# Block means of batch 0's values: eight narrow copies become two wide ones, and tile 0's second copy changes engine

## Chip, cores, metric

One core of a Trainium2 chip. The metric is the device time of one execution in microseconds (us), lower is better; the kernel before takes 511.47 us, the median of three runs (511.29 to 512.98). A core has a matrix engine (TensorE, PE in the profile, with its weight loads as PEld), a vector engine (VectorE, DVE), a scalar engine (ScalarE, ACT), a general one (GpSimd, POOL) and a queue that here only issues transfers (SyncE, SP). Each runs its own instructions in order, and waits on semaphores that the others raise.

## The reference, cut down

Attention over a local window plus block summaries, then two feed-forward parts:

```python
k_sum = k.reshape(B, H, nb, block, D).max(axis=3)
v_sum = v.reshape(B, H, nb, block, D).mean(axis=3)      # block = 32, nb = 24
scores_l = where(|i - j| < 16, scale * q @ k^T, -1e9)
scores_s = scale * q @ k_sum^T + log(block)
a = softmax(concat([scores_l, scores_s]))
x = a @ concat([v, v_sum])                              # 2 batches, 768 rows, 8 heads x 64
x = sigmoid(xr @ w_r) * (relu(xk @ w_k) ** 2 @ w_v)     # xk, xr mix each row with the one before
u = x + (relu(x^T @ w_tok1) @ w_tok2)^T
out = u + relu(u @ w_ch1) @ w_ch2
```

## The kernel before

Attention works on 6 tiles of 128 rows in each of 2 batches. A tile's scores (`s_stage`, L309) go, for each half tile of 64 queries, against 96 window keys and the 24 block maxima. DVE adds the mask and takes the minimum (L327, into `pe`), ACT takes the exponential (L329). In batch 0 the division comes at the end (L377 to L386); in batch 1 DVE makes the reciprocals (L337, L338) and POOL scales `pe` by them (L340). TensorE transposes `pe` (L346, into bank `pt`), ACT or DVE copies it out as `PT` (L349, L351), and `v_stage` (L366) multiplies it with the values.

The values that `v_stage` reads are one 120-row operand for each half tile: 96 rows of v by DMA and, above or below them, the 24 block means. In batch 0 these operands lie in `ybuf`, slot 2t for tile t's first half (means in rows 0 to 23) and slot 2t + 1 for its second (rows 96 to 119). The means themselves are made once for a batch: DVE sums blocks (L253), TensorE transposes (L260), ACT scales into `vs` (L262). `copy_sums` (L278) then puts `vs` into each operand. In batch 0 ACT copies both of tile 0 (L283), and for each of tiles 1 to 5 POOL copies one (L287) and DVE the other (L285). In batch 1 it is a DMA (L281).

Beside attention runs the first feed-forward part, `main` (L523): `ko` matmuls (L477), ReLU on ACT (L489), square on DVE (L490), a split into a high part on ACT (L491, `kh`) and a low part on POOL (L492, `kl`), and `acc` matmuls (L477). All of these matmuls are three products of high and low parts. Each weight tile is prepared by ACT (L148), DVE (L152, L158), ACT again (L160, the high part) and POOL (L161, the low part); two buffers `wf` carry it, so the L152 of a weight waits for the L161 of the second-last one. `mixed` (L461) makes the inputs `xk` on POOL and DVE (L466, L467), with a high part on ACT (L468) and a low one on DVE (L469, `xl`).

The order on each engine is not the order of the code. `attention()` and `main()` are interleaved by a credit of costs, and a scheduler then orders every engine's instructions by priorities (`ahead(...)`) and its own estimate of when each is ready; a few matmuls and weight steps are tied to one another with `behind` and `after`. Score banks (`s`) and transpose banks (`pt`) are two each, bank `ko` is one. Eight short runs of idle matmuls (`spin`, L556) stand between the first score tiles.

Of the kernel before, what the change touches and what calls it, by code (L numbers as in the profile page):

```python
# [54 lines left out]
def fused_kernel(ctx, tc, q, k, v, vt, mu, w_k, w_v, w_r, w_t1, w_t2, w_c1, w_c2, out):  # L55
    nc = tc.nc
    B, NT = q.shape[:2]
    S, DM = v.shape[1] - WINDOW * 2, v.shape[2]
# [5 lines left out]
    NB = S // BLOCK  # L64
    KD = DM // 128
    PAD = 16
    NK = 96
    NC = NB + NK
# [21 lines left out]
    ybuf = ypool.tile([128, B * NT, DM], F32, name="ybuf")  # L90
# [4 lines left out]
    r1 = pool("r1", "right")  # L95
# [114 lines left out]
    state = {}  # L210
# [64 lines left out]
    def vw_sums(b, t):  # L275
        ahead(HV if b or t == 0 else 0)(copy_sums)(b, t)

    def copy_sums(b, t):  # L278
        for j, (w, srow) in enumerate(state[b]["vw"][t]):
            if b:  # L280
                nc.sync.dma_start(w[srow:srow + NB], state[b]["vs"])  # L281
            elif t == 0:
                nc.scalar.copy(w[srow:srow + NB], state[b]["vs"])  # L283
            elif j:
                nc.vector.tensor_copy(w[srow:srow + NB], state[b]["vs"])  # L285
            else:
                nc.gpsimd.tensor_copy(w[srow:srow + NB], state[b]["vs"])  # L287

    @ahead(HL)
    def q_load(b, t):  # L290
# [575 lines left out]
```

## Time and profile before

| what | value |
|---|---|
| median of 3 runs | 511.47 us |
| profiled execution, its time | 511.19 us |
| its span | 509.4 us |
| TensorE matmul busy | 492.6 us (97%) |
| DVE, ACT, POOL busy | 249.1, 206.4, 186.4 us |

The span is the stretch in which the program's instructions run; 1.8 us lie around it. Busy shares are means over stages: attention fills the first 170 us, and the second feed-forward part and its matmuls the rest. A wait counts only where TensorE stands idle for it.

### The profile page before, as it was taken

The page shows a single profiled execution, that of the slowest core. Times are in us where ns is not written, and L with a number is a line of the kernel's source. Part 1 is how long each engine was busy: PE and PEld are TensorE (multiplying, and loading weights), DVE is VectorE, ACT ScalarE, POOL GpSimd, SP SyncE. Part 2 cuts the span into 40 slices and gives each one's busy share as a digit, 9 for nine tenths or more (in the row PEclk, how much of TensorE's full clock was granted, in tenths as well). Part 3 has the DMA queues.
Part 4 walks back from the last instruction along what each step waited for, and adds up shares of the span by engine and source line. Part 5 has one row for each costly group of instructions (what it writes and reads, how often), then busy time and mean ns, then how long its engine had stood idle before and what let it go on. Part 6 is the DMA issues. An engine that isn't in the chain of part 4 may idle for free.

```text
span 509.4 us, 7950 instructions
## 1 busy us (share of the span) xinstructions
PE 492.6 (97%) x3064; PEld 399.6 (78%) x3064; DVE 249.1 (49%) x544; ACT 206.4 (41%) x477; POOL 186.4 (37%) x250
## 2 busy tenths in 40 slices
PE   7999897999999999999999999999999999999995
PEld 3578775788888888887888888888888888888884
DVE  3789999740515174798676576343141211311112
ACT  1689655962534444556455435343110201001000
POOL 5335567971534465697734333332100000000000
PEclk9999999999999999999999999999999999999999
DMA  8999942031000660001525650000020000200002
GB/s 254 307 295 338 333 128 71 9 100 40 21 0 14 237 248 0 1 0 42 164 85 209 235 176 1 0 1 1 0 84 0 1 0 1 82 1 0 0 1 82
DMA packets 24197, 45.40 MB, mean 89 GB/s; under 512 B 2112, under 2 KB 11328, under 8 KB 24160
## 3 DMA queue, kind: packets, MB, share of 16 engines
q1 hardware_dynamic: 24160, 44.90, 28.1%
q8 instruction: 24, 0.39, 0.3%
q14 instruction: 13, 0.11, 0.1%
HBM read 41.16 MB, written 3.15 MB: 87 GB/s over the span
## 4 chain that ended last, share of the span: by engine, by line
PE 79%; DVE 9%; POOL 4%; issue 3%; ACT 2%; DMA 2%; SPq 1%; DVEq 0%; POOLq 0%; ACTq 0%
PE o L791 19%; PE go L477 19%; PE ko L477 10%; PE acc L477 10%; PE ro L477 5%; PE ho L477 3%; PE h L477 3%; PE sp L309 3%; PE pv L366 2%; DVE xk L467 2%; PE pt L346 2%; DMA xT<-in_vt_dram 1%; PE spin L556 1%; DVE wf L152 1%; PE utr L745 1%
## 5 line engine op out<-in xcount | busy, mean ns | idle before, releaser
L477 PE MATMUL go<-u,w 128*128 128x512 f32 x432 | 106.7, 393 | 0.0
L161 POOL TENSOR_TENSOR w<-wf,w 128x512 fp32r<-128x512 f32 x50 | 68.7, 1379 | 85.5 <-ACT w L160 78.8
L477 PEld LDWEIGHTS go<-u,w 128*128 128x128 f32 x432 | 80.7, 188 | 17.5
L791 PE MATMUL o<-w,gh 128*128 128x512 f32 x288 | 89.0, 395 | 0.0
L706 DVE SCALAR_TENSOR_TENSOR gl<-go,gh 128x512 fp32r<-128x512 f32 x36 | 24.9, 691 | 121.1 <-ACT gh L705 120.9
L477 PE MATMUL ko<-xh,w 128*128 128x256 f32 x384 | 77.0, 289 | 0.7 <-ACT w L160 0.6
L705 ACT ACTIVATE gh<-go 128x512 fp32r<-128x512 f32 x36 | 21.5, 597 | 128.8 <-PE go L477 128.7
L477 PEld LDWEIGHTS ko<-xh,w 128*128 128x128 f32 x384 | 61.4, 188 | 4.5 <-issue 1.3
L791 PEld LDWEIGHTS o<-w,gh 128*128 128x128 f32 x288 | 54.0, 188 | 12.1
L477 PE MATMUL acc<-w,kh 128*128 128x512 f32 x192 | 60.7, 398 | 1.9 <-ACT kh L491 1.9
L477 PE MATMUL ko<-xl,w 128*128 128x256 f32 x192 | 54.6, 284 | 1.0 <-DVE xl L469 1.0
L791 PE MATMUL o<-w,gl 128*128 128x512 f32 x144 | 55.4, 394 | 0.0
L160 ACT CAST w<-wf 128x512 fp32r<-128x512 f32 x50 | 30.9, 619 | 47.3 <-DVE wf L158 47.1
L492 POOL TENSOR_TENSOR kl<-rl,kh 128x512 fp32r<-128x512 f32 x24 | 34.5, 1437 | 34.6 <-ACT kh L491 31.2
L466 POOL TENSOR_SCALAR tmp<-xT,oms 128x256 f32<-128x256 f32 x52 | 38.1, 742 | 23.1 <-DVE xk L467 15.0
L158 DVE SCALAR_TENSOR_TENSOR wf<-wst,wf 128x512 int32<-128x512 int32 x50 | 41.4, 834 | 8.4 <-ACT wst L148 6.9
L329 ACT ACTIVATE pe<-pe,mn 128x120 f32<-128x120 f32 x96 | 36.6, 383 | 18.5 <-DVE mn L327 18.2
L477 PEld LDWEIGHTS acc<-w,kh 128*128 128x128 f32 x192 | 34.6, 188 | 9.1 <-ACT kh L491 2.4
L490 DVE TENSOR_TENSOR rl<-rl 128x512 f32<-128x512 f32 x24 | 18.9, 785 | 46.7 <-ACT rl L489 46.3
L467 DVE SCALAR_TENSOR_TENSOR xk<-xT,mus,tmp 128x256 f32<-128x256 f32 x52 | 39.2, 784 | 4.2 <-POOL tmp L466 3.8
L477 PE MATMUL acc<-w,kl 128*128 128x512 f32 x96 | 37.1, 397 | 1.1 <-POOL kl L492 1.1
L477 PEld LDWEIGHTS ko<-xl,w 128*128 128x128 f32 x192 | 36.2, 189 | 2.1 <-DVE xl L469 1.3
(85 smaller groups left out, 695.2 us busy)
## 6 DMA issues: line engine op xcount, KB each, us to landing
wst<-in_moe_w_ch_dram SPq DMA_DIRECT2D x24, 512.0 KB, 4.6
wst<-in_moe_w_k_dram SPq DMA_DIRECT2D x8, 512.0 KB, 7.6
wst<-in_moe_w_v_dram SPq DMA_DIRECT2D x8, 512.0 KB, 10.3
kw<-in_k_dram SPq DMA_DIRECT2D x12, 320.0 KB, 8.8
wst<-in_moe_w_tok_dram SPq DMA_DIRECT2D x6, 512.0 KB, 4.5
out_dram<-o SPq DMA_DIRECT2D x12, 256.0 KB, 2.0
ybuf<-in_v_dram SPq DMA_DIRECT2D x12, 192.0 KB, 9.8
vw<-in_v_dram SPq DMA_DIRECT2D x12, 192.0 KB, 2.6
```

What stands on the lines that cost most here:

```text
L158: nc.vector.scalar_tensor_tensor(wi, top, 3, wi, ALU.logical_shift_left, ALU.bitwise_or)
L160: self.rounded.append(nc.scalar.copy(hi, wf))
L161: nc.gpsimd.tensor_tensor(lo, wf, hi.bitcast(F32), ALU.subtract)
L329: nc.scalar.activation(pe, pe, AF.Exp, bias=mn[:, p:p + 1], scale=-1.0, accum_out=den[:, p:p + 1])
L466: nc.gpsimd.tensor_scalar(tmp, xT[:, d, x0 - 1:x0 - 1 + MW], om[:, d:d + 1], 1.0, ALU.mult, ALU.mult)
L467: nc.vector.scalar_tensor_tensor(xk[:, d], xT[:, d, x0:x0 + MW], mu[:, d:d + 1], tmp, ALU.mult, ALU.add)
L477: nc.tensor.matmul(o, l, r, start=(first and i == 0), stop=(last and i == 3 * n - 1))
L490: nc.vector.tensor_tensor(rl, rl, rl, ALU.mult)
L492: nc.gpsimd.tensor_tensor(lo, rl, hi.bitcast(F32), ALU.subtract)
L705: nc.scalar.activation(hi, o, AF.Relu)
L706: nc.vector.scalar_tensor_tensor(lo, o, 0.0, hi.bitcast(F32), ALU.max, ALU.subtract)
L791: nc.tensor.matmul(acc[t], l, r, start=(f == 0 and i == 0), stop=(f == nf - 1 and i == 2))
```

## The change

For batch 0, tile 0's first copy stays on ACT and its second goes to DVE; tile 1 keeps one copy on POOL and one on DVE. The copies of tiles 2 to 5 become two instructions, issued where tile 2's were: POOL writes the first-half slots of all four tiles (24 rows, 4 x 512 elements, `vs` read four times over), DVE the second-half slots. Batch 1 keeps its DMAs.

```diff
     def copy_sums(b, t):
-        for j, (w, srow) in enumerate(state[b]["vw"][t]):
-            if b:
-                nc.sync.dma_start(w[srow:srow + NB], state[b]["vs"])
-            elif t == 0:
-                nc.scalar.copy(w[srow:srow + NB], state[b]["vs"])
-            elif j:
-                nc.vector.tensor_copy(w[srow:srow + NB], state[b]["vs"])
-            else:
-                nc.gpsimd.tensor_copy(w[srow:srow + NB], state[b]["vs"])
+        vs = state[b]["vs"]
+        if b:
+            for w, srow in state[b]["vw"][t]:
+                nc.sync.dma_start(w[srow:srow + NB], vs)
+        elif t < 2:
+            (w0, r0), (w1, r1) = state[b]["vw"][t]
+            (nc.gpsimd.tensor_copy if t else nc.scalar.copy)(w0[r0:r0 + NB], vs)
+            nc.vector.tensor_copy(w1[r1:r1 + NB], vs)
+        elif t == 2:
+            rest = ybuf[:, 2 * t:2 * NT].rearrange("p (t two) n -> p t two n", two=2)
+            wide = vs.unsqueeze(1).to_broadcast([NB, NT - t, DM])
+            nc.gpsimd.tensor_copy(rest[0:NB, :, 0], wide)
+            nc.vector.tensor_copy(rest[NK:NC, :, 1], wide)
```

Behind line 292 the changed kernel's line numbers are 4 higher, so its L331 is L327 of before, its L494 is L490. On every engine the scheduler's order is another one, in places from about 28 us of the trace of before up to the end of attention. Three places follow.

ACT, as batch 0's last two tiles end. Before, the first ReLU of `main` (L489) stands behind the last two copies of attention:

```order
L160 CAST w<-wf 128x512
L148 ACTIVATE wst<-wst 128x512
L349 COPY PT<-pt 120x512
L385 COPY xT<-pv 128x4x128
L160 CAST w<-wf 128x512
L148 ACTIVATE wst<-wst 128x512
L489 ACTIVATE rl<-ko 128x512
```

With the change it stands ahead of them:

```order
L160 CAST w<-wf 128x512
L148 ACTIVATE wst<-wst 128x512
L493 ACTIVATE rl<-ko 128x512
L353 COPY PT<-pt 120x512
L389 COPY xT<-pv 128x4x128
L160 CAST w<-wf 128x512
L148 ACTIVATE wst<-wst 128x512
L495 CAST kh<-rl 128x512
```

The ReLU and the high part `kh` behind it have moved ahead, and so has the square on DVE (L490).

DVE, where batch 1's attention starts: the block maxima (L231) and what stands between them and the first masked scores of batch 1 (L327), before:

```order
L231 TENSOR_REDUCE ks<-kw 128x4x4 x2
L469 TENSOR_TENSOR xl<-xk,xh 128x1024
L231 TENSOR_REDUCE ks<-kw 128x4x4
L152 TENSOR_SCALAR wf<-wst 128x512
L158 SCALAR_TENSOR_TENSOR wf<-wst,wf 128x512
L351 COPY PT<-pt 120x512
L490 TENSOR_TENSOR rl<-rl 128x512
L253 TENSOR_REDUCE vrs<-ybuf 128x48
L158 SCALAR_TENSOR_TENSOR wf<-wst,wf 128x512
L152 TENSOR_SCALAR wf<-wst 128x512
L158 SCALAR_TENSOR_TENSOR wf<-wst,wf 128x512
L386 TENSOR_TENSOR xT<-xT,rb 128x4x128
```

And with the change:

```order
L231 TENSOR_REDUCE ks<-kw 128x4x4 x2
L473 TENSOR_TENSOR xl<-xk,xh 128x1024
L494 TENSOR_TENSOR rl<-rl 128x512
L158 SCALAR_TENSOR_TENSOR wf<-wst,wf 128x512
L152 TENSOR_SCALAR wf<-wst 128x512
L253 TENSOR_REDUCE vrs<-ybuf 128x48
L355 COPY PT<-pt 120x512
L158 SCALAR_TENSOR_TENSOR wf<-wst,wf 128x512
L331 ISA pe,mn<-sp,mask_183 128x120
L331 ISA mn 128x1
```

The last block maximum has moved ahead of the long `xl`, and the masked scores (8 pairs of such rows) ahead of two L152, one L158 and the L386.

TensorE, behind the scores of batch 1's second tile, before:

```order
L309 MATMUL sp<-kw,qT 64x120 x6
L477 MATMUL acc<-w,kh 128x512 x4
L477 MATMUL ko<-xh,w 128x256
L477 MATMUL ko<-xl,w 128x256
L477 MATMUL acc<-w,kl 128x512 x2
L477 MATMUL acc<-w,kh 128x512 x2
L477 MATMUL acc<-w,kl 128x512
L477 MATMUL acc<-w,kh 128x512 x2
L477 MATMUL acc<-w,kl 128x512
L309 MATMUL sp<-kw,qT 64x120
L346 MATMUL pt<-ident,pe 120x128 x4
```

And with the change:

```order
L313 MATMUL sp<-kw,qT 64x120 x16
L350 MATMUL pt<-ident,pe 120x128 x4
L313 MATMUL sp<-kw,qT 64x120
L350 MATMUL pt<-ident,pe 120x128
L481 MATMUL ko<-xh,w 128x256
L481 MATMUL ko<-xl,w 128x256
L350 MATMUL pt<-ident,pe 120x128 x2
L313 MATMUL sp<-kw,qT 64x120 x15
```

The first transposes of batch 1 now stand right behind the scores; the `acc` matmuls that separated them come later, and behind the rows shown follow 7 `ko` matmuls, one transpose, one score matmul of the fourth tile, 4 `acc` matmuls and 11 more scores of that tile.

## Rows read from the trace of the kernel before

**Rows 1.** Busy time by stretches: stretch, length, busy us (instructions) of PE, PEld, DVE, ACT, POOL; granted clock.

```profile
20.00:40.00 20.00, 20.00 (x219) 13.59 (x217) 15.61 (x62) 17.92 (x61) 8.83 (x10) 1.00 1.08 301
100.00:200.00 100.00, 100.00 (x827) 85.90 (x821) 41.18 (x105) 47.25 (x113) 51.13 (x68) 1.00 0.25 84
```

**Rows 2.** Timeline, TensorE's waits from 50 us: start us, length us, engine, line, [idle <-releaser].

```profile
53.20 0.39 PE L477 MATMUL ko<-xl,w 128*128 128x256 f32 x1 [1.04 <-DVE xl L469]
61.76 1.12 PE L556 MATMUL spin<-ident 128*128 128x512 f32 x2 [0.41 <-ACT rl L489]
67.56 1.19 PE L477 MATMUL acc<-w,kh 128*128 128x512 f32 x4 [0.84 <-ACT kh L491]
81.45 0.39 PE L309 MATMUL sp<-kw,qT 64*64 64x120 f32 x2 [0.87 <-issue]
82.22 0.82 PE L309 MATMUL sp<-kw,qT 64*64 64x120 f32 x18 [0.38 <-DVE mn L327]
86.26 1.20 PE L477 MATMUL acc<-w,kh 128*128 128x512 f32 x4 [1.05 <-ACT kh L491]
88.08 0.38 PE L477 MATMUL ko<-xh,w 128*128 128x256 f32 x1 [0.62 <-ACT w L160]
95.27 1.00 PE L346 MATMUL pt<-ident,pe 128*120 128x128 f32 x3 [0.28 <-POOL pe L340]
```

**Rows 3.** Timeline around the copies, as in rows 2.

```profile
22.70 3.42 DVE L285 COPY ybuf<-vs 24x512 f32<-24x512 f32 x5 [0.89 <-ACT vs L262]
22.73 3.85 POOL L287 COPY ybuf<-vs 24x512 f32<-24x512 f32 x5 [2.04 <-ACT vs L262]
24.09 1.24 ACT L283 COPY ybuf<-vs 24x512 f32<-24x512 f32 x2
27.38 0.68 DVE L351 COPY PT<-pt 120x512 f32<-120x512 f32 x1
28.48 0.97 PE L366 MATMUL pv<-PT,ybuf 120*64 120x64 f32 x13
```

**Rows 4.** The copies by tile `vs`: shortest/median/longest ns of one.

```profile
L285 DVE COPY ybuf<-vs x5: 420/826/827, 22.7 to 25.3; 24x512 f32<-24x512 f32 x5
L287 POOL COPY ybuf<-vs x5: 797/797/852, 22.7 to 25.8; 24x512 f32<-24x512 f32 x5
```

**Rows 5.** Timeline, DVE and POOL where batch 1 starts.

```profile
70.64 3.88 POOL L237 TENSOR_SCALAR kw<-ks 128x96 f32<-128x96 f32 x12 [1.77 <-DVE ks L231]
...
76.24 1.48 DVE L152 TENSOR_SCALAR wf<-wst 128x512 int32<-128x512 int32 x1 [1.19 <-POOL w L161]
77.82 1.60 DVE L158 SCALAR_TENSOR_TENSOR wf<-wst,wf 128x512 int32<-128x512 int32 x1
79.34 0.67 DVE L386 TENSOR_TENSOR xT<-xT,rb 128x512 f32<-128x512 f32 x1
...
80.35 0.60 DVE L152 TENSOR_SCALAR wf<-wst 128x512 int32<-128x512 int32 x1
82.08 0.73 DVE L467 SCALAR_TENSOR_TENSOR xk<-xT,mus,tmp 128x256 f32<-128x256 f32 x1
```

**Rows 6.** The chain that ended last, piece by piece: start us, length us, what.

```profile
83.04 1.61 PE ko L477 x12
84.65 0.58 PE sp L309 x12
```

**Rows 7.** Groups in 80 to 91 us: count, busy us, mean ns of one.

```profile
L467 DVE SCALAR_TENSOR_TENSOR xk<-xT,mus,tmp 128x256 f32<-128x256 f32 x4 | 3.4, 845 | 0.0
L158 DVE SCALAR_TENSOR_TENSOR wf<-wst,wf 128x512 int32<-128x512 int32 x3 | 3.2, 1053 | 0.0
...
L161 POOL TENSOR_TENSOR w<-wf,w 128x512 fp32r<-128x512 f32 x3 | 4.1, 1368 | 0.0
L466 POOL TENSOR_SCALAR tmp<-xT,oms 128x256 f32<-128x256 f32 x4 | 3.1, 770 | 2.1 <-DVE xT L386 1.3 <-DVE xk L467 0.7
L340 POOL TENSOR_SCALAR pe<-pe,den 128x120 f32<-128x120 f32 x4 | 2.0, 523 | 0.5 <-DVE den L338 0.5
```

## Prediction

> **What bounds the kernel now.** I read the shares by stretches first, then TensorE's waits on the timeline, then the stretch of the copies. From 100 to 200 us TensorE is busy all the time [rows 1], and it has little idle time behind that: what moves attention by a microsecond moves the end only if TensorE's waits before 100 us grow or shrink. From 50 us on the eight largest are 1.04, 0.41, 0.84, 0.87, 0.38, 1.05, 0.62 and 0.28, 5.5 us together [rows 2]. Each ends on DVE, ACT or POOL, none on a transfer. Between 20 and 40 us, where the copies are, TensorE is busy for 20.00 of 20 us at the full clock, 1.00 of 2.4 GHz [rows 1]: what DVE, ACT or POOL save there has no wait to shorten. So the copies can hardly gain by themselves. They can lose by coming late, and they gave the scheduler a reason to order attention anew, which is the larger part of this change.
>
> **The copies.** ACT loses one copy, 1.24 for two, so 0.6 [rows 3]; TensorE waits for nothing there, so it brings nothing. DVE gets six copies' worth of data in place of five, in three instructions; POOL keeps five, in two. Before, ten copies ran in pairs: POOL's five took 3.85, or 0.77 each, DVE's five 3.42 [rows 3]. One DVE copy took 0.42 and the others 0.83, though they are alike [rows 4]: a DVE copy waits out a POOL copy. The 0.77 of a pair holds a POOL part and a DVE part; the latter is at most 0.42, which leaves POOL 0.35 or more, and at most its 0.80. I take 0.45 and 0.32, because DVE's 0.42 holds a start that lies beside POOL's end.
>
> Now DVE's two narrow copies end at about 22.70 + 0.42 + 0.77 = 23.9. POOL's wide one has stood ready by then since its narrow copy ended (22.73 + 0.85 = 23.6), and goes first: 4 x 0.45 = 1.8, to 25.7. DVE's wide one follows, 4 x 0.32 = 1.3, to 27.0, where the block of before ended at 26.1. Behind it on DVE stand four masked scores, a weight step and the copy of PT, which ended at 28.06 and is read by the `pv` at 28.48 [rows 3]: slack 0.42. 0.9 later less 0.42 is a wait of 0.45 on TensorE. Ends: none, if DVE's wide copy goes first (23.9 + 1.3 = 25.2) or beside POOL's; 1.9, if POOL's part is all of its 0.80 (3.2, so 28.4). I take 0.45, since the pairs of before could not come every 0.77 with a part of 0.80.
>
> The Trainium skill speaks against the wide copies: "SBUF — State Buffer", section "SBUF: two separate sides", has DVE in its two-port mode and POOL take one port pair as an exclusive lock for a whole instruction, so four times the length locks the other out for four times as long. The alternating 0.42 and 0.83 agree [rows 4]. By that rule the sum holds the 0.45, and without it (side by side) it would be 0.45 lower.
>
> **The order from 50 to 82 us.** The first ReLU on ACT, its square on DVE and `kh` stand earlier; this ends the waits of 0.41 and 0.84 [rows 2]. The last block maximum stands ahead of `xl`, and the masked scores of batch 1's first tile ahead of L152, L158, L386 and L152; the waits of 0.87 and 0.38 of the second tile's scores on those go too [rows 2]. Together 2.50. The wait of 1.04 for `xl` halves, as `xl` now stands ahead of four masked scores, but four transposes that ran beside this wait (about 0.5, by the 1.00 of three that waited, an upper end) come afterwards: nothing. New: `kl` on POOL queues behind the twelve sums of 3.88 [rows 5], which start earlier but as one block; an estimate of 0.6, between 0 and 1.2. Net 2.50 - 0.6 - 0.45 = 1.45 gained when TensorE ends the second tile's scores. That was at 85.23 [rows 6], of which 1.61 was `ko` work that now comes later, so it is now 83.6 - 1.45 = 82.2.
>
> **The order from 82 to 100 us.** Here attention is pulled ahead of `main`. The waits of before there, 1.05, 0.62 and 0.28, lose their cause: 1.95 gone [rows 2]. But between the second tile's scores and the first transposes of batch 1 stood 20 matmuls that covered the way over DVE, ACT and POOL; now nothing does. I walk that way with the mean lengths of this stretch [rows 7].
>
> DVE ended the first tile's masked scores at 82.1; the 4.35 of L152, L158, L386 and L152 that stood ahead and 1.19 of idle time go [rows 5], the 0.9 of the copies comes: 77.5. Then two L152 (0.60) and two L158 (1.05), 3.3, to 80.8 with the reciprocals (small, left out). POOL scales four `pe` at 0.52, to 82.9: the four transposes end 0.3 late. DVE goes on with L386 and eight masked scores, 0.67 and 1.5 (82.08 less the end of L386, 80.01, less the 0.60 between), to 83.0. POOL does two L466 at 0.77, to 84.4, then the next `pe`, to 84.9: the next transpose, due at about 83.2, waits 1.7, and the two behind it some 0.4. TensorE then has 15 scores and 7 `ko` matmuls, about 2.1 by the paces of rows 6, and stands before the fourth tile's score at about 88.2. That needs DVE's third tile: from 83.0, two L467 at 0.85 and a square (taken as an L386, 0.67), 85.4; L152 waits until POOL's L161 returns its buffer (86.0 + 1.37 = 87.4), and with 0.60, L158's 1.05 and four masked scores of 0.75 it is 89.8: a wait of 1.6. Four `acc` matmuls of 1.2 later [rows 2] the other eleven scores wait for 0.75 + 0.60 + 0.85 on DVE, 92.0, where TensorE stands at 91.0: 1.0. Sum 0.3 + 1.7 + 0.4 + 1.6 + 1.0 = 5.0, the upper end. The lower is 0: with short lengths throughout DVE and POOL can be ahead. I take two thirds, 3.3, because the mean of 1.05 for an L158 comes from one long one among three. Net loss here 3.3 - 1.95 = 1.35. Behind that, `ko` matmuls cover everything again, as they did from 100 us on.
>
> **Sum.** The profiled execution took 511.19, 0.3 below the median of 511.47. 511.19 - 1.45 + 1.35 = **511.1**: no change that a measurement of this kernel could tell, which takes over 0.3% (1.5 us, so under 509.9 or over 513.0). With all ends low: 511.19 - 2.50 - 1.95 = 506.7; with all high (1.9, 1.2, 5.0): 511.19 - 2.50 - 1.95 + 8.1 = 514.8.
>
> **Rivals.** *Faster:* the early order pays and DVE keeps ahead, with new waits from 82 us on of 1.5 in place of 3.3: 509.3. For it: eight waits are known to go, while the new ones are worked out. Against: DVE is in the path of each new one. Chance 0.30.
>
> *Slower:* DVE's fixed order in 82 to 92 us. An L152 or L158 that meets POOL takes 1.48 or 1.60 against 0.60 [rows 5], and TensorE's third and fourth score tiles stand behind two of each. With two more long ones than I count, 2 x 0.95 on the upper end of 5.0, the sum is 511.1 + 1.7 + 1.9 = 514.7; it decides as soon as the new waits pass 5.2 (513.0). For it: nothing stands between to cover. Against: before, TensorE lost only 1.95 there beside the same instructions. Chance 0.22.
>
> *Long POOL copy:* POOL holds the port for 4 x 0.80 and the `pv` waits 1.9, not 0.45: 512.6. Against it: pairs every 0.77. Chance 0.08, still no change. The Trainium skill would give it: "GPSIMD Engine Reference", section "Elementwise — side-by-side cycle accounting", has 512 one-input elements at 769 ns, an estimate of 3.1 for the wide copy; rows 3 speak against it.
>
> **How the numbers follow.** Forecast 0.40 and the long copy 0.08 make no change 0.48; faster 0.30, slower 0.22. The range goes from 508.5, between the faster rival and the low end, to 513.6, between the threshold and the slower rival; about 0.1 is left out on each side.
>
> **What would show it.** Right: DVE's wide copy starts when POOL's ends and the block ends near 27.0; a wait of some 0.4 at the second `pv`; no wait at `spin` or the first `acc`; masked scores of batch 1's first tile done near 77.5; waits of transposes on L340 and of scores on L327 between 82 and 92; TensorE full behind 100. Wrong: new waits before 82 us, waits on a transfer of q or v for batch 1, or TensorE idle again behind 100 us.

## The result, and the profile after

The changed kernel takes 517.55 us (median of 5 runs, 515.16 to 520.07), the kernel before in the same session 511.47: a ratio of 1.0113 [1.0091, 1.0135]. It is slower by 1.1%, and above the range of 508.5 to 513.6. The profiled execution took 518.69, with a span of 516.9 us against 509.4. Executions of one kernel differ in their granted clock as well, and a trace is one of them: of eighteen of the kernel before, timed beside e5 to e7, the six with a mean clock of 0.998 took 510.9 to 511.6 us and the eight with 0.992 took 513.0 to 513.6.

The page of the changed kernel, first the span, then busy time of TensorE, then the granted clock in 40 slices of 12.9 us:

```profile
span 516.9 us, 7960 instructions
...
PE 497.5 (96%) x3064; PEld 404.3 (78%) x3064; DVE 248.3 (48%) x542; ACT 205.7 (40%) x476; POOL 185.0 (36%) x247
...
PEclk9999998799999999999999999999999999999999
```

TensorE ran the same 3064 matmuls. It was busy for 497.5 us, 4.9 more than before, and idle for 19.4, 2.6 more: together the 7.5 of the span. More busy time for the same work is new, and the row of the clock shows where: two slices of lower clock, from 77.5 to 103.4 us. The shares by stretches, TensorE alone (columns: stretch, its length, busy time and matmuls, granted clock, DMA share, GB/s):

```profile
70.50:73.80 3.30, 0.04 (x1) 1.00 0.01 2
73.80:75.20 1.40, 1.40 (x33) 1.00 0.00 0
75.20:82.00 6.80, 6.00 (x16) 0.50 0.00 0
82.00:93.00 11.00, 8.72 (x128) 1.00 0.41 115
93.00:95.70 2.70, 1.52 (x6) 1.00 0.00 0
95.70:102.50 6.80, 6.80 (x40) 0.50 0.00 0
```

Before, all of this was at 1.00. Now TensorE stands still from 70.5 to 73.8, and 1.4 us after it has started again it has 0.50, 1.2 GHz, for 6.8 us; then it has two waits between 91 and 95.7, and again 0.50 for 6.8 us. In the two stretches it was busy for 6.00 + 6.80 = 12.8 us, work of 6.4 at full clock: 6.4 us lost. With 2.6 of additional idle time that is 9.0, of which 1.5 came back elsewhere in TensorE's 497 us; that part was not traced.

TensorE's waits (who waits, for whom, us in total, times, longest):

```profile
PE sp L313 <- POOL kw L237: 4.4, 2, 3.3
PE sp L313 <- DVE mn L331: 3.0, 2, 1.8
PE acc L481 <- POOL kl L496: 1.9, 2, 1.1
...
PE pv L370 <- DVE PT L355: 0.6, 1, 0.6
PE ko L481 <- DVE xl L473: 0.5, 1, 0.5
...
PE sp L313 <- PE pt L350: 0.5, 1, 0.5
```

Of the eight waits of [rows 2] the one on `xl` is halved, and the other seven are gone. One of 3.3 us is new and far larger than any of them: batch 1's first scores wait for a sum of `kw` on POOL. (`ks` are the block maxima, the reference's `k_sum`; an instruction at L237 writes them beside the window keys in `kw`, twice for each tile, and the text calls these twelve instructions of a batch its sums. The other wait on `kw`, of 1.2, is batch 0's; `mn` are the minima that DVE writes as it masks the scores.) The timeline around it, POOL, then DVE, then TensorE (start, us, engine, line, operation, and in brackets the idle time before it and who ended it):

```profile
71.04 5.81 POOL L237 TENSOR_SCALAR kw<-ks 128x96 f32<-128x96 f32 x12
...
70.86 1.21 DVE L473 TENSOR_TENSOR xl<-xk,xh 128x1024 fp32r<-128x1024 f32 x1
72.00 0.68 DVE L494 TENSOR_TENSOR rl<-rl 128x512 f32<-128x512 f32 x1
72.60 0.68 DVE L158 SCALAR_TENSOR_TENSOR wf<-wst,wf 128x512 int32<-128x512 int32 x1
73.20 0.42 DVE L152 TENSOR_SCALAR wf<-wst 128x512 int32<-128x512 int32 x1
73.54 1.74 DVE L253 TENSOR_REDUCE vrs<-ybuf 128x48 f32<-128x1536 f32 x1
...
73.80 1.28 PE L313 MATMUL sp<-kw,qT 64*64 64x120 f32 x32 [3.26 <-POOL kw L237]
...
78.15 1.22 PE L481 MATMUL acc<-w,kl 128*128 128x512 f32 x2 [0.80 <-POOL kl L496]
```

And all sums of that line (duration in ns: least, median, longest):

```profile
L237 POOL TENSOR_SCALAR kw<-ks x24: 265/276/2710, 12.2 to 76.6; 128x96 f32<-128x96 f32 x24
```

23 of the 24 sums take about 0.27 us. The first of batch 1 takes 2.71: from 71.04 to 73.75, as long as DVE runs `xl`, the square `rl`, L158 and L152 without a pause; it ends when DVE has come to a reduction. Before, `xl` ran ahead of the last block maximum, and the twelve sums took 3.88 [rows 5], not 5.81, the longest of all sums 0.762.

Last the copies, DVE, POOL and the `pv` behind them, in the same columns:

```profile
24.49 2.91 DVE L291 COPY ybuf<-vs 24x2048 f32<-24x2048 f32 x1
...
24.23 2.08 POOL L290 COPY ybuf<-vs 24x2048 f32<-24x2048 f32 x1
...
29.39 0.97 PE L370 MATMUL pv<-PT,ybuf 120*64 120x64 f32 x13 [0.58 <-DVE PT L355]
```

POOL's wide copy goes first and ends at 26.31, DVE's ends 1.09 later: one after the other, as forecast, 2.08 and 1.09 where the forecast has 1.8 and 1.3, with a wait of 0.58 against the 0.45 forecast.

### The profile page after: what moved, and what is told of

Same layout as the page of the kernel before. It is cut to its first block, busy times and chain, and to the rows that moved or that the text cites. A ratio compares the mean times of both kernels' runs of the same rounds, so it can differ in the third digit from the quotient of the medians.

```text
span 516.9 us, 7960 instructions
## 1 busy us (share of the span) xinstructions
PE 497.5 (96%) x3064; PEld 404.3 (78%) x3064; DVE 248.3 (48%) x542; ACT 205.7 (40%) x476; POOL 185.0 (36%) x247
## 4 chain that ended last, share of the span: by engine, by line
PE 79%; DVE 11%; POOL 2%; DMA 2%; ACT 2%; issue 2%; SPq 1%; DVEq 0%; ACTq 0%
PE o L795 19%; PE go L481 19%; PE acc L481 12%; PE ko L481 11%; PE ro L481 4%; PE ho L481 3%; PE h L481 3%; PE pv L370 2%; DVE xk L471 2%; DMA xT<-in_vt_dram 2%; PE sp L313 2%; DVE pe L331 1%; PE pt L350 1%; DVE wf L152 1%; POOL kw L237 1%
## 5 line engine op out<-in xcount | busy, mean ns | idle before, releaser
L161 POOL TENSOR_TENSOR w<-wf,w 128x512 fp32r<-128x512 f32 x50 | 67.3, 1351 | 82.1 <-ACT w L160 79.5
L481 PE MATMUL acc<-w,kh 128*128 128x512 f32 x192 | 62.6, 415 | 0.0
L494 DVE TENSOR_TENSOR rl<-rl 128x512 f32<-128x512 f32 x24 | 19.6, 815 | 61.0 <-ACT rl L493 61.0
L158 DVE SCALAR_TENSOR_TENSOR wf<-wst,wf 128x512 int32<-128x512 int32 x50 | 40.7, 820 | 4.0 <-ACT wst L148 2.4
L481 PEld LDWEIGHTS acc<-w,kh 128*128 128x128 f32 x192 | 36.0, 196 | 7.8 <-issue 0.2
L481 PE MATMUL acc<-w,kl 128*128 128x512 f32 x96 | 38.5, 422 | 1.9 <-POOL kl L496 1.9
L471 DVE SCALAR_TENSOR_TENSOR xk<-xT,mus,tmp 128x256 f32<-128x256 f32 x52 | 35.6, 714 | 3.5 <-POOL tmp L470 3.2
```

The lines of the kernel that those rows point to most:

```text
L158: nc.vector.scalar_tensor_tensor(wi, top, 3, wi, ALU.logical_shift_left, ALU.bitwise_or)
L161: nc.gpsimd.tensor_tensor(lo, wf, hi.bitcast(F32), ALU.subtract)
L471: nc.vector.scalar_tensor_tensor(xk[:, d], xT[:, d, x0:x0 + MW], mu[:, d:d + 1], tmp, ALU.mult, ALU.add)
L481: nc.tensor.matmul(o, l, r, start=(first and i == 0), stop=(last and i == 3 * n - 1))
L494: nc.vector.tensor_tensor(rl, rl, rl, ALU.mult)
```

## The experiments

The theory after the result, **O**: not the copies but the new order costs the time. It puts four DVE instructions beside the first sum of `kw`, which holds the sum up; TensorE waits, and then loses its clock. Rivals: **W**, the wide copies cost it; **I**, the idle time alone counts and the clock falls for another reason; **V**, DVE's work sets this stretch whichever way TensorE waits. Each kernel was timed in 5 rounds beside the kernel before (511.4 to 512.9 us in these sessions). All of them:

| run | edit | us | ratio to before | mean clock |
|---|---|---|---|---|
| changed kernel | | 517.55 | 1.0113 [1.0091, 1.0135] | 0.985 |
| e1 | before, tile 0's second copy on DVE | 517.51 | 1.0095 [1.0071, 1.0118] | 0.984 |
| e2 | changed, wide copies cut up | 517.63 | 1.0102 [1.0084, 1.0120] | 0.981 |
| e3 | changed, last maximum behind `xl` | 521.32 | 1.0173 [1.0152, 1.0193] | 0.990 |
| e4 | changed, matmuls in the gap | 514.66 | 1.0045 [1.0029, 1.0062] | 0.993 |
| e5 | changed, two sums on ACT | 513.86 | 1.0034 [1.0015, 1.0054] | 0.987 |
| e6 | changed, tile 0 on ACT | 517.49 | 1.0099 [1.0074, 1.0124] | 0.985 |
| e7 | e6 and e5 together | 515.20 | 1.0059 [1.0036, 1.0082] | 0.990 |
| e8 | before, two tiles wide | 511.74 | 0.9997 [0.9984, 1.0010] | 0.996 |
| e9 | changed, twelve sums on ACT | 511.68 | 0.9988 [0.9974, 1.0001] | 0.991 |
| e10 | e5, later sums behind `kl` | 516.80 | 1.0089 [1.0070, 1.0108] | 0.990 |
| e11 | e9, two matmuls added | 511.37 | 0.9985 [0.9972, 0.9997] | 0.994 |
| e12 | e9, four matmuls added | 516.53 | 1.0094 [1.0076, 1.0111] | 0.998 |

**e1, e2 and e8: the order or the wide copies.** e1 takes the kernel before and moves one copy, from ACT to DVE:

```diff
-            elif t == 0:
+            elif t == 0 and j == 0:
                 nc.scalar.copy(w[srow:srow + NB], state[b]["vs"])
```

> The kernel before with one edit: tile 0's second block-mean copy on VectorE instead of ScalarE; the other ten copies stay narrow and where they were. Its instructions stand on every engine in the order of the changed kernel, but for the copies. Theory O (the loss is the new order: the first kw sum of batch 1 now runs beside two-input VectorE instructions and takes 2.7 us, TensorE waits 3.3 us at its scores and its granted clock then falls to 0.50): 515.5 to 518.5, a wait of 2.5 to 3.5 us at sp near 73 us, clock 0.50 for some 5 us after it. Theory W (the wide copies cost it, by holding SBUF or by delaying pv): 511 to 512, no such wait.

e2 takes the changed kernel and cuts its wide copies up:

```diff
-            nc.gpsimd.tensor_copy(rest[0:NB, :, 0], wide)
-            nc.vector.tensor_copy(rest[NK:NC, :, 1], wide)
+            for u in range(t, NT):
+                (w0, r0), (w1, r1) = state[b]["vw"][u]
+                nc.gpsimd.tensor_copy(w0[r0:r0 + NB], vs)
+                nc.vector.tensor_copy(w1[r1:r1 + NB], vs)
```

> The changed kernel with its two wide copies cut into four narrow ones each, at the same place and on the same engines; TensorE's and SyncE's orders are those of the changed kernel. Theory O: 515.5 to 518.5, as the changed kernel, with the same two stretches at clock 0.50; the wait at the second pv falls from 0.58 to under 0.5. Theory W: 511 to 512.5.

e8 is the kernel before, but for tiles 4 and 5, whose four narrow copies become two wide ones. The part of its kernel that makes them (cut: above it, tiles 0 to 3 are copied as before):

```python
        if t == 4:
            T = 4
            rest = ybuf[:, 2 * T:2 * NT].rearrange("p (t two) n -> p t two n", two=2)
            wide = vs.unsqueeze(1).to_broadcast([NB, NT - T, DM])
            nc.gpsimd.tensor_copy(rest[0:NB, :, 0], wide)
            nc.vector.tensor_copy(rest[NK:NC, :, 1], wide)
```

> The kernel before, with the copies of the last two tiles (not four) made by one wide instruction each on GpSimd and VectorE, issued with tile 4's; tiles 0 to 3 as before, so tile 0's two stay on ScalarE. TensorE's, ScalarE's and SyncE's orders are those of the kernel before. Theory O: as the kernel before, ratio 0.997 to 1.003, clock 1.00 from 60 to 120 us. Theory W (wide copies cost by themselves): 2 to 4 us slower, half of the change's loss for half of its wide tiles.

e1 has no wide copy and loses all the same; its trace has the sum of 2.71 and the wait again. In e2 they are there too, the sum with 2.71. e8 has wide copies, and no loss. The first two fences are the timelines of e1 and of e2, the third the shares of e8 by stretches, TensorE alone:

```profile
74.83 1.28 PE L309 MATMUL sp<-kw,qT 64*64 64x120 f32 x32 [3.26 <-POOL kw L237]
```

```profile
74.55 2.10 PE L313 MATMUL sp<-kw,qT 64*64 64x120 f32 x32 [3.27 <-POOL kw L237]
```

```profile
60.00:110.00 50.00, 45.33 (x440) 1.00 0.30 84
```

W has fallen: two wide tiles cost nothing that can be measured, and the changed kernel with its four is not slower than e1 and e2 without, as the intervals show. The wait of 0.58 behind the copies is gone in e2, as expected, and in e1; but both traces are at 0.50 from about 18 to 22 us, and TensorE comes to that place more than 1 us later, so this does not price the wide copies. e2's narrow copies end at 27.66, no earlier than the wide ones (27.40). The smallest part of the change is enough for the loss: one copy of tile 0 on another engine, from which the scheduler derives another order for the rest of attention. It is not the only part that is enough: in e6, below, the wide copies alone give a third order and a loss of the same size.

**e5 and e9: free the sums.** e5 takes the first two sums of batch 1 from POOL to ACT, and the order stays but for two places behind 90 us:

```diff
+            if b and t == 0:
+                nc.scalar.copy(st["kw"][t][:, :, o:o + NB], st["ks"])
+            else:
                 nc.gpsimd.tensor_scalar(st["kw"][t][:, :, o:o + NB], st["ks"], 1.0, 1.0, ALU.mult, ALU.mult)
```

> The changed kernel with batch 1's first two kw sums on ScalarE instead of GpSimd (which the two-input VectorE instructions beside them hold up); TensorE's, VectorE's and SyncE's orders stay but for two places after 90 us. Theory O: the first kw sum takes 0.3 to 0.5 us instead of 2.7, the wait at batch 1's first scores falls from 3.3 to 0.8 to 1.6 us, the granted clock stays 1.00 from 75 to 82 us: 2 us of waiting and some 3 us of half clock come back, 511.5 to 514. Rival V (VectorE's back-to-back work sets the time of this stretch, whichever way TensorE waits): the wait moves behind the scores (kl, mn), 515 to 517. Theory W (the wide copies): 517 to 518.

513.86, 3.7 less than the changed kernel: the total is inside O's range. But the clock is not as expected. e5's timeline, ACT, POOL, TensorE, and below it its sums on POOL:

```profile
71.09 0.45 ACT L238 COPY kw<-ks 128x96 f32<-128x96 f32 x2 [0.84 <-DVE ks L231]
...
71.22 4.76 POOL L240 TENSOR_SCALAR kw<-ks 128x96 f32<-128x96 f32 x10 [0.22 <-DVE ks L231]
75.95 1.78 POOL L499 TENSOR_TENSOR kl<-rl,kh 128x512 fp32r<-128x512 f32 x1
...
71.41 1.21 PE L316 MATMUL sp<-kw,qT 64*64 64x120 f32 x32 [0.76 <-ACT kw L238]
73.49 1.20 PE L484 MATMUL acc<-w,kh 128*128 128x512 f32 x4 [0.87 <-ACT kh L498]
...
77.78 1.22 PE L484 MATMUL acc<-w,kl 128*128 128x512 f32 x2 [2.85 <-POOL kl L499]
```

```profile
L240 POOL TENSOR_SCALAR kw<-ks x22: 268/272/2637, 11.5 to 75.7; 128x96 f32<-128x96 f32 x22
```

The scores wait 0.76, not 3.26. The hold-up has moved with the queue: the first sum that is left on POOL now takes 2.64, and `kl`, behind ten sums, is late by 2.85; the clock goes to 0.50 there (76 to 83 us). So e9 moves the other ten as well (the condition becomes `if b:`):

> The kernel of e5 with batch 1's other ten kw sums on ScalarE as well, so that none is left on GpSimd ahead of kl; the orders of TensorE and VectorE are those of e5. In e5 TensorE waited 2.85 us for that kl, which ten held-up sums (4.8 us) stood ahead of. Theory O: the sums take about 0.25 us each on ScalarE, kh comes 1 to 1.5 us later, kl 1 to 2 us earlier; the waits between 71 and 78 us fall from 4.5 to about 3.5 us in sum, none over 2.5, and the clock may stay 1.00: 510.5 to 513.5. Rival V (VectorE sets this stretch): 513.5 to 515, as e5.

511.68, a ratio of 0.9988 where the changed kernel has 1.0113: taking twelve small sums out of DVE's way gives back the whole loss. V has fallen. On ACT the twelve take 0.267 each; e9's timeline, ACT, POOL, TensorE:

```profile
70.28 2.17 ACT L238 COPY kw<-ks 128x96 f32<-128x96 f32 x12 [0.85 <-DVE ks L231]
...
73.05 1.30 POOL L499 TENSOR_TENSOR kl<-rl,kh 128x512 fp32r<-128x512 f32 x1 [2.85 <-ACT kh L498]
...
70.60 1.21 PE L316 MATMUL sp<-kw,qT 64*64 64x120 f32 x32 [0.76 <-ACT kw L238]
73.02 1.21 PE L484 MATMUL acc<-w,kh 128*128 128x512 f32 x4 [1.21 <-ACT kh L498]
```

With TensorE's and DVE's orders almost those of the changed kernel, its two later waits on `mn`, 1.79 and 1.18, are gone too: they came of the sums on POOL as well, by the late start or by POOL's longer queue, which no run tells apart. Not all of the clock is back: e9's trace keeps one stretch of 6.8 us at 0.50 (shown with e11), where the changed kernel has two; TensorE is idle for 14.1 us in it, in the kernel before for 16.8.

**e4: the clock by itself.** The sums stay held up; six matmuls of 256 columns fill the gap:

```diff
             nc.tensor.transpose(vp[:NB, p], st["vr"][:, p], ident)
+            if b and p == 1:
+                for _ in range(6):
+                    nc.tensor.matmul(vp[:, 2:4], ident, ident.unsqueeze(1).to_broadcast([128, 2, 128]), start=True, stop=True)
```

> The changed kernel with six additional matmuls of 256 columns on TensorE right ahead of batch 1's first scores (into a part of the bank that is overwritten later), some 2.6 us at full clock; the kw sums, xl and the copies are unchanged up to there, behind it the order differs. Theory O with the clock as its larger part: the first kw sum still takes about 2.7 us and the scores start no earlier, but TensorE is idle under 1.2 us there and its granted clock stays 1.00 from 75 to 82 us; 512.5 to 516. Rival I: the clock is 0.50 there all the same, 516 to 519. Theory W: 517 to 519.

514.66, 2.9 less than the changed kernel, with additional work on TensorE. Its shares by stretches, TensorE alone:

```profile
70.00:74.00 4.00, 3.33 (x30) 1.00 0.00 0
74.00:76.00 2.00, 1.25 (x13) 1.00 0.00 0
76.00:82.00 6.00, 5.02 (x49) 1.00 0.00 0
82.00:90.00 8.00, 4.67 (x27) 0.70 0.07 16
```

Its sums, and its wait at batch 1's first scores:

```profile
L237 POOL TENSOR_SCALAR kw<-ks x24: 268/272/2712, 11.8 to 75.4; 128x96 f32<-128x96 f32 x24
...
72.65 0.88 PE L316 MATMUL sp<-kw,qT 64*64 64x120 f32 x18 [0.67 <-POOL kw L237]
```

The first sum still takes as long, but TensorE waits 0.67, and from 76 to 82 us the clock is 1.00 where the changed kernel has 0.50. I has fallen for this stretch: with work in the place of the wait the clock stays. The other executions agree: the mean clock of e4's six is 0.990 to 0.995, of the changed kernel's five 0.982 to 0.989. Behind 82 us the order differs, a wait of 3.33 for a ReLU on ACT comes (82 to 90 us: busy 4.67 of 8), and with it a lower clock.

**e3: another order of the two.** The last block maximum goes behind `xl` instead of ahead of it (cut: `xls` collects the `xl` subtractions):

```diff
-        nc.vector.tensor_reduce(st["ks"][:, :, n * t:n * t + n], keys, AX.X, ALU.max)
+        m = nc.vector.tensor_reduce(st["ks"][:, :, n * t:n * t + n], keys, AX.X, ALU.max)
+        if b and t == NT - 1:
+            behind(m, xls[1:2])
```

> The changed kernel with VectorE's last key maximum of batch 1 put behind the 1.2 us xl subtraction instead of ahead of it, so that the kw sums start after xl; the copies are unchanged. Theory O: the first kw sum under 1.6 us, the wait at batch 1's first scores under 1.5 us, the granted clock 1.00 from 75 to 82 us; 511.5 to 515 (the later wait, on the maxima mn, may stay). Rival I (the idle time alone counts, the clock falls for another reason): 0.50 stays, 514 to 516. Theory W: 517 to 518.

521.32: a miss of all three. e3's timeline:

```profile
73.07 3.83 POOL L240 TENSOR_SCALAR kw<-ks 128x96 f32<-128x96 f32 x12 [1.77 <-DVE ks L232]
...
73.76 0.42 PE L316 MATMUL sp<-kw,qT 64*64 64x120 f32 x4 [2.82 <-POOL kw L240]
...
86.39 0.97 PE L353 MATMUL pt<-ident,pe 128*120 128x128 f32 x2 [2.64 <-POOL pe L347]
```

The sums are fast again (at most 0.694 us), as O says, but they start 2.0 us later, and TensorE waits 2.82 all the same: a sum that comes late costs what a sum that is held up costs. The 2.82 left the clock at 1.00 up to 84 us; with the wait of 2.64 up to 86.4, which this order brings, came 0.50.

**e6 and e7: tile 0 back on ACT.** Both wide copies stay, tile 0's second copy returns:

```diff
-            nc.vector.tensor_copy(w1[r1:r1 + NB], vs)
+            (nc.vector.tensor_copy if t else nc.scalar.copy)(w1[r1:r1 + NB], vs)
```

> The changed kernel with tile 0's second copy back on ScalarE; the two wide copies stay as the change has them. The order on every engine is a third one, in which VectorE has the xl subtraction right behind the last key maximum as in the changed kernel, but TensorE has twelve ko matmuls (1.4 us) between the last transposes and batch 1's first scores. Theory O: the wait at these scores is 1.3 to 2.2 us, the clock stays 1.00 there, 511 to 514.5. Theory W: 516.5 to 518.5.

e7 adds e5's edit to it:

> The kernel of e6 (wide copies, both copies of tile 0 on ScalarE) with batch 1's first two kw sums on ScalarE as well; apart from these two the order on every engine is that of e6. Theory O: the wait at batch 1's first scores under 0.5 us, 0.5 to 2 us less than e6. Rival V: the same time as e6 within 0.5 us, with the wait elsewhere.

e6 takes 517.49, above O's range and inside W's, though e8 and e2 exclude W. Its sum is held up for 2.11 us, but twelve `ko` matmuls cover that, and there is no wait at batch 1's first scores. What e6 loses, it loses at other places that its order makes, near 50 and 83 us, each with a stretch at 0.50 behind it (52 to 55 and 86 to 93 us); its trace has a third such stretch from 18 to 22 us, ahead of the copies, as those of e1, e2, e5 and e11 have and those of the kernel before and the changed kernel do not. e6's timeline:

```profile
50.85 0.65 PE L350 MATMUL pt<-ident,pe 128*120 128x128 f32 x4 [1.41 <-DVE xT L390]
52.12 1.65 PE L370 MATMUL pv<-PT,ybuf 120*64 120x64 f32 x13 [0.62 <-DVE PT L355]
...
83.75 0.32 PE L350 MATMUL pt<-ident,pe 128*120 128x128 f32 x1 [1.83 <-POOL pe L344]
```

e7 is 2.3 faster than e6 (the intervals of their ratios just overlap) although TensorE did not wait for these sums in e6. Its waits at the same places are 1.4 and 1.6, and its second stretch at 0.50 is about half as long (85 to 89 us); near 20 us it has none. So O's wait held, where e6 had none either; the gain is a little over its range and came at other places, in the two traces as less time at 0.50.

**e10: the later sums behind `kl` on POOL.** To e5's edit it adds (cut: `kls` collects the `kl` instructions):

```diff
+                g = nc.gpsimd.tensor_scalar(st["kw"][t][:, :, o:o + NB], st["ks"], 1.0, 1.0, ALU.mult, ALU.mult)
+                if b:
+                    behind(g, kls[-1:])
```

> The kernel of e5 with the other ten kw sums of batch 1 put, on GpSimd, behind the kl instructions that were emitted ahead of them instead of in a row ahead of kl; batch 1's second tile of scores then comes 10 to 20 us later, with ko and acc matmuls in its place. Theory O: no wait over 1.5 us between 70 and 80 us, clock 1.00 from 60 to 100 us, 509 to 512.5. Rival L (batch 1's attention becomes late and TensorE waits for it behind 100 us): 513 to 518.

516.80: the total is rival L's, and TensorE does wait for batch 1's attention, but ahead of 100 us and not behind it. No wait over 0.9 between 70 and 80 us, as expected; but TensorE waits seven times from 81 to 98 us, 0.26 to 1.19 each, and the clock is at 0.50 from 84 to 91 us.

**e11 and e12: more activity ahead of e9's last slow stretch.** e9 keeps one, of which the shares show, TensorE alone:

```profile
75.20:82.00 6.80, 6.56 (x85) 1.00 0.08 17
82.00:84.50 2.50, 2.38 (x16) 0.99 0.21 49
84.50:91.30 6.80, 6.80 (x43) 0.50 0.48 150
```

```diff
         pt = bank("pt", 2, [128, NP, 128], "pt")
+        if z["u"][:2] == (1, 0):
+            for _ in range(1):
+                nc.tensor.matmul(pt[:, :2], ident, ident.unsqueeze(1).to_broadcast([128, 2, 128]), start=True, stop=True)
```

e12 has `range(2)`.

> The kernel of e9 with one additional matmul of 256 columns on TensorE ahead of each of batch 1's first two sets of transposes pt (into their own bank, which the transposes then overwrite), near 80 to 84 us: 2 x 0.43 us of work at full clock where TensorE had short pauses between small matmuls ahead of the one stretch at clock 0.50 (84.4 to 91.2 us) that e9 has left. The order stays but for a few rows. Theory O with the clock: 0.50 does not come between 80 and 100 us, some 3 us come back less at most 0.9 of additional work: 508.5 to 510.5. Rival K (the clock falls by something else than pauses there): 0.50 stays, 511.5 to 513.

> As e11, with two matmuls of 256 columns ahead of each of the two sets of transposes (1.7 us in all); the order behind 80 us differs from e9's. Theory O with the clock: no stretch at 0.50 from 80 to 90 us; what a new order brings behind it is not known, 508.5 to 516. Rival K: 0.50 from 84 to 91 us as in e9.

e11: 0.50 does not come between 80 and 100 us, as expected, but the time is 511.37, not 510.5 or less; a wait of 0.91 on `mn` has come in, and its profiled execution has 0.50 from 18 to 22 us, where e9's had none. Nor does the trace show that the added matmuls removed e9's stretch: four of e9's own twelve executions have a mean clock of 0.998 or 0.999, and 6.8 us at 0.50 alone would lower it by 0.007. Between O and K this run does not decide. e12 has the clock at 1.00 throughout attention, and takes 516.53: TensorE waits little, and is busy for 499.0 us. Of the 6.4 more than before the added matmuls are 2.2 (the trace has each of the four as two) and `pv` of batch 1 is up to 2.7; the busy time of a group also counts what overlaps its neighbours. e12's groups, then the same `pv` group of the kernel before:

```profile
L376 PE MATMUL pv<-PT,vw 120*64 120x64 f32 x192 | 10.2, 228 | 0.0
...
L354 PE MATMUL pt<-ident 128*128 128x256 f32 x8 | 2.2, 392 | 0.0
```

```profile
L366 PE MATMUL pv<-PT,vw 120*64 120x64 f32 x192 | 7.5, 226 | 0.0
```

The group of the same 192 matmuls is busy for 36% longer. In e12 an `acc` stands directly ahead of a `pv` thirteen times, before three times (counted in the trace), and such a `pv` starts 0.40 us behind the `acc`, where another `acc` starts 0.23 behind it (means of 105 to 185 us). Ten more such places at 0.17 are 1.7 us. The changed kernel has nine, and 9.4 us of `pv`; so has e9, which is as fast as the kernel before. That an order costs in this third way, without a wait, is read from the traces; no run changes these places alone.

## Why the prediction was wrong

**The copies: right.** One wide copy behind the other, 0.58 of waiting for 0.45; and e8 and e2 say that it is nothing that can be told at the end.

**Waits that go: right.** 0.41, 0.84, 0.87, 0.38, 1.05, 0.62 and 0.28 went, 1.04 became 0.5. One was misread: the prediction has each of them end on DVE, ACT or POOL, but the row of 0.87 names `issue`, no engine.

**The order from 50 to 82 us: wrong, and this is the step that failed.** It said: "New: `kl` on POOL queues behind the twelve sums of 3.88 [rows 5], which start earlier but as one block; an estimate of 0.6, between 0 and 1.2." For `kl` that was near, 0.80. But the 3.88 was the length of the sums beside the DVE instructions of before [rows 5]. The change had put `xl`, a square, L158 and L152 beside them, as the order of DVE showed, and the first sum took 2.71. The walk then began with DVE's masked scores and never asked when the scores themselves could start: TensorE came to them earlier, because its waits were gone, at 70.5, and stood for 3.26. With the sums on ACT (e5, e9) 0.76 of that is left. The prediction knew how DVE and POOL hold each other up; it used it for the copies and not for the sums. The Trainium skill ("SBUF — State Buffer", section "SBUF: two separate sides") names DVE instructions with two inputs in SBUF among those that lock a POOL instruction out. The trace agrees for `xl`, `rl` and L158, which have two, and shows besides that POOL did not get its turn between four instructions in a row, the last of which, L152, has one tensor input.

**A term that was missing: TensorE's clock.** The sum counted idle time at its own length. Of the 9.0 us lost, 6.4 were TensorE at 0.50 behind its waits. In their traces e9 gives back the waits and one of the two stretches at 0.50, e4 the first wait, which added matmuls fill, and the stretch behind it. With the sums out of the way e9 comes to the forecast, 0.9988 of the kernel before where 511.1 is 0.9993, but with a stretch at half clock that the forecast did not have; so that is no proof of its other terms. "TensorE: Matmul & The Clock Gate" of the Trainium skill, section "HAM oscillation — how this bites in real kernels", warns that gaps in TensorE's work bring its clock down. The changed kernel agrees, while e9 fell to 0.50 behind 9.3 us in which TensorE was busy for 8.94 (75.2 to 84.5).

**The order from 82 to 100 us: right in its sum, by luck.** It had 3.3; the waits are 0.49, 1.79 and 1.18, 3.46 together. The 1.6 and 1.0 for the scores of the fourth tile are the 1.79 and 1.18; the 2.4 for transposes did not come. But the walk had the second tile's scores end at 82.2, and they ended at 86.6, late by the wait and the half clock above; and e9, with almost the same order, has none of these waits. The waits belong to the sums on POOL and not to the order that the walk priced.

**The rivals.** The slower one, 514.7 by DVE's fixed order behind 82 us, had the sign and not the mechanism. The long POOL copy did not come, 2.08 against its 3.2, and e1 has the loss without any wide copy. "New waits before 82 us" stood among the signs of a wrong prediction, without a price.

**What stays open.** When the clock falls. A wait of 2.82 left it (e3), one of 2.64 did not (e3), and in e9 it fell without one over 1.21, in some of its executions and not in all. Why e7 gains on e6 at sums that nobody waited for. And why e3 is the slowest: TensorE is busy for 501.5 us there, 8.9 more than before, of which its one stretch at 0.50 (6.12 us of work between 86 and 93 us) is about 3.

## What to carry to other kernels

If a scheduler orders the program, the smallest edit can move everything behind it; the edit's own cost then says little. Take each moved instruction and ask what now runs beside it on the engine that can hold it up (here DVE, for POOL), before its old length is used again. And a new wait of TensorE can cost about twice its length: here 3.26 us of waiting stood ahead of 6.00 us of work at half clock, 3.0 us lost, while a wait of 2.82 in e3 stood ahead of none.

For this kernel: e9 and e11, the changed kernel with batch 1's sums on ACT, are 1.2 to 1.3% faster than the changed kernel, and at 0.9988 and 0.9985 about the kernel before, within what can be told.

## What the hardware showed unexpectedly

- POOL's sum of 0.27 us was held up by four DVE instructions in a row and took 2.71 (2.64 in e5): it got in between none of them. On ACT the same sum took 0.267 beside the same instructions.
- At half clock TensorE was counted busy, so that the loss looks like work: 497.5 against 492.6 us with the same 3064 matmuls. The mean clock of a run is not a measure of its time either: e12 had the highest, 0.998, and was as slow as the changed kernel.
- A `pv` behind an `acc` started 0.40 us behind it in e12, an `acc` behind an `acc` 0.23; the 192 `pv` matmuls of batch 1 were busy, beside their neighbours in part, for 7.5, 9.4 and 10.2 us with three, nine and thirteen changes from `acc` to `pv`.
